# Halves of the first stage moved beside the third stage, the bias sum moved ahead of the difference, and the seam's casts moved

## The chip, the core and the metric

One core of one Trainium2 chip runs the program. The metric is the device time of one execution in microseconds (us); the median of several executions is compared.

## The reference

```python
X = np.fft.rfft(x, axis=1)                    # x: 8 x 3072 x 256
Yr = Xr @ w_r - Xi @ w_i + b_r                # 256 x 256 weights
Yi = Xr @ w_i + Xi @ w_r + b_i
Y = softshrink(Yr, 0.01) + 1j * softshrink(Yi, 0.01)
y = np.fft.irfft(Y, n=3072, axis=1)           # -> 24576 tokens x 256
h = y @ w_in                                  # 256 x 2048
g = where(h >= 1, h, where(h <= -1, 0, (h + 1) ** 2 / 4))
out = g @ w_out                               # 2048 x 256
```

## The kernel before

The Fourier transform of length 3072 is done as 48 x 64, as matmuls with constant matrices. **First stage** (`stage1`, line 213): a "half" is four rows of one batch; four small matmuls on quarters of the array write banks A and B (one buffer each), and two ScalarE copies (line 228) take them to `zst`, which SyncE stores to `z_d` with four transfers (`store_z`, line 230). **Second stage** (`stage2`, line 246) and **mixing** run in units: `UN` = 96 units, `NU` = 12 a batch. Second-stage matmuls write a bank of tag D (two buffers). ScalarE copies the imaginary part (`split_X_hi`, line 270) and casts the whole to `Xh` (`round_X`, line 277). VectorE forms the difference in place (`difference`, line 294), ScalarE casts it to `Xdh` (line 312), VectorE forms the low parts `Xl` (line 306) and `Xdl` (line 313). `mix_shared` (six matmuls) and `mix_rest` (twelve) multiply by the weights into a bank of tag C (two buffers; all of line 320). Between them VectorE adds `bias_i` to the shared part (`take_shared`, line 336; in the first unit of a batch also one row, line 338), and afterwards adds the sum to the bank (`add_bias`, line 350). ScalarE and VectorE shrink the result (`above`, line 355; `shrink`, line 359). **Third stage** (`stage3`, line 378, matmuls of line 368): one for two units, in odd units, into the two banks of tag E, copied by ScalarE (line 382) and stored to `u_d`. **Fourth stage** (`stage4`, line 488, `half4`): back to tokens, through banks A and B, eight parts for the first batch beside the unit loop, with ScalarE copies (line 516). Operands of the feed-forward part are cast by `prep_split_hi` (ScalarE) and `prep_split_lo` (VectorE, line 560), in four parts; part 0 and 1 come from the fourth stage's output, 2 and 3 from sums on GpSimd.

The unit loop is lines 767 to 856, and the order of each engine's queue is the order of the calls (`manual_schedule`). In iteration u stand: `mix_shared(u-2)`, `difference(u-1)` and its casts, `take_shared(u-2)`, `above(u-3)`, `Xl` and `Xdl` of u-1, `shrink(u-3)`, one weight step, in odd u `stage3(u-5)`, the halves of this unit, a part of the fourth stage if u is in `U4`, one weight step, `stage2(u)` and its copies, `mix_rest(u-2)`, one weight step, `add_bias(u-2)`. At the head of the iteration SyncE issues the stores of the halves done so far, `load_z(u+2)` and one `load_x`.

Weight steps (`weight_steps`, line 468) turn float64 weights to pairs of float32 numbers from unit 12 on, three steps a unit, so that one of 32 tiles takes two units. In even units they are the VectorE steps of lines 415, 420 and 422 and two ScalarE steps (418, 419); in odd units those of lines 424 and 426, a GpSimd product (431) and the split of the tile before (`split_weights`, line 437): for every second one of the first 16 a ScalarE cast of `winh` (line 465) and a GpSimd subtraction (466), for each of the last 16 a cast of `wout` (line 443).

Which halves fall due comes from these lines; an even unit takes one of those due, an odd unit leaves one:

```python
lo, hi = (min(NH, NJ + (max(0, k - 1) if k <= NJ else NJ + 2 * (k - NJ) // 3)) for k in (u, u + 1))
hs_u = due[: 1 if not odd else max(0, len(due) - 1)]
```

Of the kernel before, what the change touches and what calls it, by code (L numbers as in the profile page):

```python
# [103 lines left out]
def tile_fft_mix_moe(  # L104
    ctx: ExitStack, tc: tile.TileContext, x, x_first, w_r, w_i, b_r, b_i, w_in, w_out, c1, c2, t_f, t_i, out
):
    nc = tc.nc
# [7 lines left out]
    NU = G // 2  # L115
# [48 lines left out]
    def split(eng, hi, lo, src):  # L164
        eng.tensor_copy(hi, src)
        eng.tensor_tensor(out=lo, in0=src, in1=hi.bitcast(F32), op=ALU.subtract)
# [46 lines left out]
    def stage1(h, tags, copies):  # L213
        a = xin.pop(h)
        ps = [pools["ps"].tile([P, HT, D], F32, tag=k, bufs=2 if k == "C" else 1, name="ps_f1") for k in tags]
        for k, e in QUARTERS:
            rows = slice(k * HP, k * HP + R1)
            nc.tensor.matmul(  # L218
                ps[k][e * HP : (e + 1) * HP],
                lhsT=c1_sb[rows, Q:],  # L220
                rhs=a[rows, e * HT : (e + 1) * HT, :],
                start=True,
                stop=True,
                tile_position=(k * HP, e * HP),
            )
        for k, copy in enumerate(copies):
            z = zst[h, k] = first_st.tile([P, HT, D], F32, tag="zst", bufs=5, name="zst")
            copy(z, ps[k])
# [31 lines left out]
    def both(ps):  # L260
        return (ps[:, :, c].rearrange("p d g s -> p d (g s)") for c in range(2))

    def split_X_hi(u):
        ps = xp[u]
        _, im = both(ps)
        if u == 0:
            dp[u] = fold.tile([P, 2, D], F32, tag="yb", name="im")[:, :, :P]
        else:
            dp[u] = mixing.tile([P, ND, P], F32, tag="Xd", name="Xd")
        nc.scalar.copy(dp[u], im)  # L270
        if u > 0:
            round_X(u)

    def round_X(u):
        ps = xp[u]
        hi = mixing.tile([P, ND, 2, 2, R2], F32R, tag="Xh", bufs=2, name="Xh")
        nc.scalar.copy(hi, ps)
        xp[u] = ps, hi
# [19 lines left out]
    def split_first(u):  # L298
        if u in first_col:
            e = first_col.pop(u)  # L300
            split(nc.vector, *(a[:, :, 0:1] for a in e0), e)
# [32 lines left out]
    def take_shared(u):  # L334
        ps = yp[u]
        nc.vector.tensor_tensor(out=shift[:, 1, :], in0=ps[:, 0, :], in1=bias_i, op=ALU.add)
        if u % NU == 0:
            nc.vector.tensor_tensor(out=shift[0:1, 1, :], in0=ps[0:1, 0, :], in1=shift[0:1, 0, :], op=ALU.add)
# [173 lines left out]
    def stage4_out(c, copies):  # L512
        hb, m = divmod(c, JH // JT)
        to = yt[hb][:, :, :, m * JT : (m + 1) * JT].rearrange("p d (r h) j -> p d r h j", h=2)
        for h, (copy, ps) in enumerate(zip(copies, ps4.pop(c), strict=True)):
            copy(to[:, :, :, h, :], ps.rearrange("p d j r -> p d r j"))

    def bank(tag, bufs=1):
        return pools["ps"].tile([P, 2, BANK // 2], F32, tag=tag, bufs=bufs, name="ps_i2")
# [21 lines left out]
    def split_slices(i, part):  # L541
        hb, k = divmod(i, NK)
        if part == 0:
            sl, src = slice(0, 1), halves_of(i)[0][0].rearrange("p q j -> p (q j)")
        elif part == 1:
            sl, src = slice(1, 3), yt[hb][:, 1, k * QT : (k + 1) * QT, :].rearrange("p q j -> p (q j)")
        else:
            at = 2 * part - 4
            sl, src = slice(3 + at, 5 + at), raw_t[i][:, at : at + 2].rearrange("p o q j -> p (o q j)")
        return src, *(a[:, sl, :].rearrange("p o n -> p (o n)") for a in ops[i])  # L550

    def prep_split_hi(i, part):
        if part == 0:
            ops[i] = [pools[f"ops{i % 2}"].tile([P, 7, TH], F32R, tag=f"op{k}", name=f"op{k}") for k in "hl"]
        src, hi, lo = split_slices(i, part)
        nc.scalar.copy(hi, src)

    def prep_split_lo(i, part):
        src, hi, lo = split_slices(i, part)
        nc.vector.tensor_tensor(out=lo, in0=src, in1=hi.bitcast(F32), op=ALU.subtract)  # L560
        if part == 3:
            del raw_t[i]
            if i % NK == NK - 1:
                del yt[i // NK]
# [115 lines left out]
    UN = B * NU  # L680

    def halves(u):

        lo, hi = (min(NH, NJ + (max(0, k - 1) if k <= NJ else NJ + 2 * (k - NJ) // 3)) for k in (u, u + 1))
        return range(lo, hi)
# [7 lines left out]
    with tc.manual_schedule():  # L693
# [61 lines left out]
        def half4(tags="AB"):  # L755
            c = next(four4)
            stage4(c, [bank(k, 2 if k == "D" else 1) for k in tags])
            stage4_out(c, [nc.scalar.copy] * 2)

        U4 = (UN - 8, UN - 6, UN - 4, UN - 3, UN)  # L760

        U_IN = UN - NU + 2

        WU = 12
        due = []
        used = NX + 1
        for u in range(UN + 3):
            odd = u % 2
            due.extend(h for h in halves(u) if h > NX + 1)
            hs_u = due[: 1 if not odd else max(0, len(due) - 1)]  # L770
            del due[: len(hs_u)]
            at = lambda lag: 0 <= u - lag < UN
            weights = more_weights if WU <= u < 85 else lambda: None
            while (stored, 0) in zst:
                store_z(stored)
                stored += 1
            if at(6) and not odd:
                store_u(u - 6)
            if u == NU:
                wout = keep.tile([P, NF, 2, D], F32R, tag="wout", name="wout")  # L780
            if 0 < u < NU - 3:
                load_t(2 * u + 6, 2 * u + 8)
            if 0 < u <= NU:
                load_ti(u - 1)
            if u == WU - 1:
                load_weights(0)
                load_weights(1)
            if u == 10:
                nc.sync.dma_start(c2_sb, c2)
            if NU <= u + 2 < UN:  # L790
                assert stored >= NJ * ((u + 2) // NU + 1)
                load_z(u + 2)
            if xs < min(NH, used + AHEAD):
                load_x(xs)
                xs += 1
            if at(2):
                mix_shared(u - 2)
            if u == 2:
                take_shared(0)
                split_first(0)  # L800
            if at(1):
                difference(u - 1)
                rest = split_difference(u - 1)
                if u == 1:
                    round_X(0)
            if at(2) and u > 2:
                take_shared(u - 2)
            if at(3):
                above(u - 3)
            if at(1):  # L810
                if u > 1:
                    split_X_lo(u - 1)
                rest()
                if u == 1:
                    split_X_lo(u - 1)
                    first_col[0] = minus_sum(*first_col[0])
                else:
                    split_first(u - 1)
            if at(3):
                shrink(u - 3)  # L820
            weights()
            if at(5) and odd:
                stage3(u - 5)
            for h in hs_u:
                stage1(h, "AB", [nc.scalar.copy] * 2)
                used += 1
            if u in U4:
                half4()
            weights()
            if u == UN + 1:  # L830
                half4("DD")
            if u < UN:
                stage2(u)
                split_X_hi(u)
            if u == 1:
                stage1(NX + 1, "AB", [nc.scalar.copy] * 2)
                used += 1
            if at(2):
                mix_rest(u - 2)
                weights()  # L840
                add_bias(u - 2)
            if u == U_IN:
                assert not due and stored == NH
                for _ in ws:
                    pass
                first_st.release()
                pools["in"] = right("in")
                pools["in"].tile([P, 24], F32, name="edge")
                pools["ops0"] = right("ops0")
                for c in range(2):  # L850
                    load_u(c)
            if u == UN - 2:
                prep_sums(0)
            for part in {UN - 2: (0,), UN - 1: (1,), UN: (2, 3)}.get(u, ()):
                prep_split_hi(0, part)
                prep_split_lo(0, part)
        mixing.release()
        pools["ops1"] = right("ops1")
        pools["ps"].release()
# [21 lines left out]
        for n in range(NUNIT):  # L881
            i, p = divmod(n, NP)
            part = p - 4 if i + 1 < NT and p >= 4 else None
# [137 lines left out]
```

## Time and profile before

| | before |
|---|---|
| median of 3 runs | 2567.1 us (2567.05 to 2567.39) |
| the profiled execution | 2565.8 us, its span 2564.0 us |
| TensorE busy | 2553.1 us (100% of the span) |
| VectorE busy | 2061.7 us (80%) |
| ScalarE busy | 1693.1 us (66%) |
| GpSimd busy | 133.5 us (5%) |
[...]

The unit loop fills the first 490 us of the span; the feed-forward part (lines 881 to 974) the rest. In the profile PE is TensorE, PEld its weight load, DVE VectorE, ACT ScalarE, POOL GpSimd and SP SyncE. Busy times are taken over whole spans, and an engine's queue is followed in a timeline. Matmuls overlap, and their ends are modelled; so TensorE's time is read from the starts.

### The profile page before, as it was taken

What the parts mean: (1) busy time and instruction counts of PE and PEld (TensorE: products, weight loads), DVE (VectorE), ACT (ScalarE), POOL (GpSimd) and SP (SyncE); (2) the same over time, 40 slices, a digit from 0 to 9 for tenths busy, and PEclk for the clock granted to TensorE, in tenths of its full rate; (3) what the DMA queues carried; (4) which work ended last, traced back from release to release, by engine and by line L of the source; (5) the groups of instructions that cost most, each with busy time, mean ns of one, the idle gap of its engine ahead of it and who ended that gap; (6) DMA issues with size and microseconds to landing.
All of it is one profiled execution on the core that took longest, in us unless ns stands there. A gap on an engine that the chain in (4) does not pass through costs nothing.

```text
span 2564.0 us, 48556 instructions
## 1 busy us (share of the span) xinstructions
PE 2553.1 (100%) x19512; PEld 2459.6 (96%) x19512; DVE 2061.7 (80%) x3246; ACT 1693.1 (66%) x2713; POOL 133.5 (5%) x144
## 2 busy tenths in 40 slices
PE   9999999999999999999999999999999999999998
PEld 8888888899999999999999999999999999999998
DVE  5788886688888888888888888888888888888886
ACT  6777776666666666666666666666666666666665
POOL 2243320000000000000000000000000000000000
PEclk9999999999999999999999999999999999999999
DMA  9988775300111111111111111111111111111001
GB/s 247 276 243 241 236 228 157 113 13 13 26 26 26 26 26 26 26 26 26 26 26 25 25 25 25 25 25 25 25 25 25 25 25 25 25 25 25 13 15 23
DMA packets 195345, 160.30 MB, mean 63 GB/s; under 512 B 117296, under 2 KB 167088, under 8 KB 195120
## 3 DMA queue, kind: packets, MB, share of 16 engines
q1 hardware_dynamic: 193312, 156.73, 24.8%
q8 instruction: 153, 2.51, 0.4%
q10 hardware_dynamic: 1808, 0.48, 0.1%
q14 instruction: 72, 0.59, 0.1%
HBM read 84.78 MB, written 72.35 MB: 61 GB/s over the span
## 4 chain that ended last, share of the span: by engine, by line
PE 98%; DMA 1%; DVE 0%; ACT 0%; issue 0%; SPq 0%
PE acc L644 41%; PE ps_X L583 16%; PE ps_Y L583 10%; PE ps_mix L320 8%; PE ps_Z L583 5%; PE ps_V L583 5%; PE ps_f L252 4%; PE ps_i L368 4%; PE ps_i L501 2%; PE ps_f L218 2%; DMA xin<-in_x 0%; DMA t_sb<-in_t 0%; DMA xin<-in_x_first 0%; DVE h L617 0%; DVE h L602 0%
## 5 line engine op out<-in xcount | busy, mean ns | idle before, releaser
L644 PE MATMUL acc<-gh,wout 128*128 128x384 f32 x4096 | 1202.4, 334 | 0.0
L644 PEld LDWEIGHTS acc<-gh,wout 128*128 128x128 f32 x4096 | 754.0, 188 | 0.0
L612 ACT ACTIVATE r<-h,half 128x768 f32<-128x768 f32 x512 | 481.5, 940 | 368.9 <-DVE h L602 368.9
L644 PE MATMUL acc<-gl,wout 128*128 128x384 f32 x2048 | 684.0, 334 | 0.1
L627 DVE TENSOR_TENSOR gl<-h,gh 128x768 fp32r<-128x768 f32 x512 | 488.7, 955 | 113.1 <-ACT gh L622 85.2
L596 ACT COPY snap<-ps_X 128x384 f32<-128x384 f32 x768 | 370.0, 482 | 301.7 <-PE ps_X L583 301.0
L617 DVE SCALAR_TENSOR_TENSOR h<-h,r 128x768 f32<-128x768 f32 x512 | 486.8, 951 | 32.2 <-ACT r L612 0.3
L622 ACT CAST gh<-h 128x768 fp32r<-128x768 f32 x512 | 429.3, 839 | 1.4 <-DVE h L617 1.4
L602 DVE CUSTOM_DVE_ANT_0 h<-ps_Y,snap 128x384 f32<-128x384 f32 x512 | 283.4, 554 | 128.4 <-PE ps_Y L583 128.2
L644 PEld LDWEIGHTS acc<-gl,wout 128*128 128x128 f32 x2048 | 384.4, 188 | 0.5 <-DVE gl L627 0.5
L583 PE MATMUL ps_X<-oph,winh 128*128 128x384 f32 x768 | 260.3, 339 | 0.6 <-ACT snap L596 0.6
L583 PE MATMUL ps_X<-opl,winh 128*128 128x384 f32 x768 | 256.6, 334 | 0.0
L583 PE MATMUL ps_X<-oph,winl 128*128 128x384 f32 x768 | 256.6, 334 | 0.0
L602 DVE CUSTOM_DVE_ANT_0 h<-ps_Z,snap 128x384 f32<-128x384 f32 x256 | 142.3, 556 | 103.5 <-ACT snap L596 103.4
L583 PE MATMUL ps_Y<-oph,winh 128*128 128x384 f32 x512 | 171.1, 334 | 0.1
L583 PE MATMUL ps_Y<-oph,winl 128*128 128x384 f32 x512 | 171.0, 334 | 0.0
L583 PE MATMUL ps_Y<-opl,winh 128*128 128x384 f32 x512 | 171.0, 334 | 0.0
L583 PEld LDWEIGHTS ps_X<-oph,winh 128*128 128x128 f32 x768 | 144.1, 188 | 3.5 <-ACT snap L596 1.6
L583 PEld LDWEIGHTS ps_X<-opl,winh 128*128 128x128 f32 x768 | 144.2, 188 | 0.0
L583 PEld LDWEIGHTS ps_X<-oph,winl 128*128 128x128 f32 x768 | 144.1, 188 | 0.0
L350 DVE TENSOR_TENSOR y<-ps_mix,shift 128x512 f32<-128x512 f32 x96 | 66.3, 690 | 95.5 <-PE ps_mix L320 95.4
L602 DVE CUSTOM_DVE_ANT_0 h<-ps_V,snap 128x384 f32<-128x384 f32 x256 | 139.9, 546 | 0.0
(124 smaller groups left out, 3789.5 us busy)
## 6 DMA issues: line engine op xcount, KB each, us to landing
uin<-u_d SPq DMA_DIRECT2D x128, 192.0 KB, 4.1
out<-ot SPq DMA_DIRECT2D x504, 48.0 KB, 2.0
u_d<-ust SPq DMA_DIRECT2D x47, 512.0 KB, 3.6
xin<-in_x SPq DMA_DIRECT2D x112, 192.0 KB, 4.3
z_d<-zst SPq DMA_DIRECT2D x224, 96.0 KB, 2.5
zin<-z_d SPq DMA_DIRECT2D x84, 256.0 KB, 3.8
wraw<-in_moe_w_in SPq DMA_DIRECT2D x16, 256.0 KB, 4.9
wraw<-in_moe_w_out SPq DMA_DIRECT2D x16, 256.0 KB, 4.5
```

The costliest lines, as they stand in the source:

```text
L252: nc.tensor.matmul(ps[:, d, :, gi, :], lhsT=z[:, gi, d * P : (d + 1) * P], rhs=t_sb[:, 2 * v + gi, :].rearrange("p (c s) -> p c s", c=2), ...
L320: nc.tensor.matmul(out, lhsT=a[:, d], rhs=wm[nm, k][:, d, :], start=start and n == 0, stop=n == 3 * ND * len(pairs) - 1, skip_group_check= ...
L350: nc.vector.tensor_tensor(out=y, in0=yp[u], in1=shift, op=ALU.add)
L368: nc.tensor.matmul(ps[gi][:, k, :], lhsT=ti_sb[rows, v + k, c, :], rhs=y[rows, c, :], start=c == 0 and k == 0, stop=c == 1, tile_position= ...
L583: nc.tensor.matmul(ups[to], lhsT=win[a][p][:, w, :], rhs=mv[:, m, :], start=start and k == 0, stop=k == 2, skip_group_check=True,)
L596: nc.scalar.copy(snaps[n][:, at, :], ups["X"])
L602: nc.vector._custom_dve(TENSOR_ADD_SAT, out=hs[n][:, to, :], in0=ups[a], in1=snaps[n][:, at, :], s0=FLT_MAX, s1=-1.0)
L612: nc.scalar.activation(rs[n][:, of(f)], hs[n][:, of(f)], AF.Square, bias=half, scale=0.5)
L617: nc.vector.scalar_tensor_tensor(out=h, in0=h, scalar=1.0, in1=r, op0=ALU.max, op1=ALU.min)
L622: nc.scalar.copy(gs[n, f][0], hs[n][:, of(f)])
L627: nc.vector.tensor_tensor(out=gl, in0=hs[n][:, of(f)], in1=gh.bitcast(F32), op=ALU.subtract)
L644: nc.tensor.matmul(acc[i, q], lhsT=wout[:, 2 * p + f, a, e * P : (e + 1) * P], rhs=gs[n, f][k][:, 1 - t, :], start=p == 0 and f == 1 and ( ...
```

## The change

It touches the unit loop alone. From unit 12 (`NU`) on, an even unit takes no halves and an odd unit takes all that are due. Where there is more than one, the first goes ahead of the third stage, and the others stay behind it. In even units from 12 on `take_shared` goes ahead of `difference`. The first-batch parts of the fourth stage move from units 88, 90, 92, 93, 96 to 89, 91 (one ahead of the third stage and one behind it), 93 and 96. Of the operand casts at the end of the loop, the ScalarE cast of part 1 goes ahead of `round_X` in unit 95, the VectorE cast of part 1 to unit 96 and those of parts 2 and 3 to unit 97.

```diff
@@ split_X_hi
         nc.scalar.copy(dp[u], im)
+        if u == UN - 1:
+            prep_split_hi(0, 1)
         if u > 0:
             round_X(u)
@@ unit loop
-        U4 = (UN - 8, UN - 6, UN - 4, UN - 3, UN)
+        U4 = (UN - 7, UN - 5, UN - 3, UN)
+        prep_lo = {UN: (1,), UN + 1: (2, 3)}
...
-            hs_u = due[: 1 if not odd else max(0, len(due) - 1)]
+            late = u >= NU
+            hs_u = due[: (0 if not odd else len(due)) if late else (1 if not odd else max(0, len(due) - 1))]
...
+            if at(2) and late and not odd:
+                take_shared(u - 2)
             if at(1):
                 difference(u - 1)
                 rest = split_difference(u - 1)
...
-            if at(2) and u > 2:
+            if at(2) and u > 2 and (odd or not late):
                 take_shared(u - 2)
...
             weights()
+            if late and len(hs_u) > 1:
+                stage1(hs_u.pop(0), "AB", [nc.scalar.copy] * 2)
+                used += 1
+            if u == UN - 5:
+                half4()
+            if u in prep_lo:
+                for part in prep_lo[u]:
+                    prep_split_lo(0, part)
             if at(5) and odd:
                 stage3(u - 5)
...
-            for part in {UN - 2: (0,), UN - 1: (1,), UN: (2, 3)}.get(u, ()):
+            for part in {UN - 2: (0,), UN: (2, 3)}.get(u, ()):
                 prep_split_hi(0, part)
-                prep_split_lo(0, part)
+                if part == 0:
+                    prep_split_lo(0, part)
```

## Rows read from the trace of the kernel before

**Rows 1.** Windows view: stretch, length, busy us of each engine, clock, DMA.
```profile
300.00:400.00 100.00, 100.00 (x812) 81.21 (x805) 82.50 (x180) 72.12 (x148) 29.23 (x30) 1.00 0.74 218
```
**Rows 2.** Timeline of PE, 330 to 345: start us, length us, engine, line, operation.
```profile
333.09 0.28 PE L320 MATMUL ps_mix<-wm_ih,Xdh 128*128 128x256 f32 x1
...
338.23 0.28 PE L320 MATMUL ps_mix<-wm_ih,Xdh 128*128 128x256 f32 x1
...
339.03 1.09 PE L218 MATMUL ps_f<-xin,c_sb 48*64 48x512 f32 x8
...
342.47 0.28 PE L320 MATMUL ps_mix<-wm_ih,Xdh 128*128 128x256 f32 x1
```
**Rows 3.** Timeline of PE in an even unit with neither half nor third stage.
```profile
417.06 0.28 PE L320 MATMUL ps_mix<-wm_ih,Xdh 128*128 128x256 f32 x1
...
417.77 1.05 PE L252 MATMUL ps_f<-t_sb,zin 128*128 128x128 f32 x8
418.67 0.39 PE L320 MATMUL ps_mix<-wm_bh,Xh 128*128 128x256 f32 x1
...
420.19 0.28 PE L320 MATMUL ps_mix<-wm_ih,Xdh 128*128 128x256 f32 x1
```
**Rows 4.** Timeline of PE in an odd unit: third stage, half, second stage.
```profile
284.23 2.00 PE L368 MATMUL ps_i<-y,ti_sb 64*128 64x256 f32 x16
286.16 1.09 PE L218 MATMUL ps_f<-xin,c_sb 48*64 48x512 f32 x8
287.18 1.16 PE L252 MATMUL ps_f<-t_sb,zin 128*128 128x128 f32 x8
```
**Rows 5.** Timeline of DVE in the even unit of rows 2; in brackets idle time before.
```profile
338.43 0.69 DVE L350 TENSOR_TENSOR y<-ps_mix,shift 128x512 f32<-128x512 f32 x1 [0.57 <-PE ps_mix L320]
339.04 0.41 DVE L294 TENSOR_TENSOR Xd<-ps_f,Xd 128x256 f32<-128x256 f32 x1
339.37 0.41 DVE L336 TENSOR_TENSOR shift<-ps_mix,bias_i 128x256 f32<-128x256 f32 x1
...
340.63 0.68 DVE L359 SCALAR_TENSOR_TENSOR y<-y,over 128x512 f32<-128x512 f32 x1
...
341.76 0.29 DVE L422 TENSOR_SCALAR scl<-scl 128x256 uint32<-128x256 uint32 x1
342.68 0.69 DVE L350 TENSOR_TENSOR y<-ps_mix,shift 128x512 f32<-128x512 f32 x1 [0.62 <-PE ps_mix L320]
```
**Rows 6.** Timeline of ACT in the same even unit and the odd one behind it.
```profile
339.80 0.72 ACT L355 ACTIVATE over<-y,lam 128x512 f32<-128x512 f32 x1
...
343.73 0.41 ACT L312 CAST Xdh<-Xd 128x256 fp32r<-128x256 f32 x1 [0.59 <-DVE Xd L294]
...
344.67 0.39 ACT L443 CAST wout<-both 128x256 fp32r<-128x256 f32 x1
```
**Rows 7.** Timeline of ACT: a first-column unit, a `winh` cast, and a half's copies.
```profile
255.21 0.41 ACT L312 CAST Xdh<-Xd 128x256 fp32r<-128x256 f32 x1 [0.98 <-DVE Xd L296]
...
158.46 0.92 ACT L465 CAST winh<-wpair 128x896 fp32r<-128x896 f32 x1
...
287.30 1.08 ACT L228 COPY zst<-ps_f 128x512 f32<-128x512 f32 x2
```
**Rows 8.** Timelines of POOL and of DVE at 139 us.
```profile
139.50 2.16 POOL L466 TENSOR_TENSOR winl<-wpair,winh 128x896 fp32r<-128x896 f32 x1 [4.54 <-ACT winh L465]
...
139.58 2.22 DVE L424 TENSOR_SCALAR scl<-scl 128x256 uint32<-128x256 uint32 x1
```
**Rows 9.** Timeline of PE: units 86 and 96.
```profile
434.30 1.05 PE L252 MATMUL ps_f<-t_sb,zin 128*128 128x128 f32 x8
435.64 0.39 PE L320 MATMUL ps_mix<-wm_bh,Xh 128*128 128x256 f32 x1 [0.29 <-DVE shift L338]
...
483.79 0.39 PE L320 MATMUL ps_mix<-wm_bh,Xh 128*128 128x256 f32 x1 [1.17 <-DVE shift L336]
```
**Rows 10.** Timeline of SP: the issue of one half's four stores.
```profile
287.91 1.72 SPq L236 DMA_DIRECT2D z_d<-zst  x4
```

## The prediction

> **What bounds the kernel now.** Read the stretches first, then the timelines of one pair of units, engine by engine. In the unit loop TensorE is busy all the time while VectorE and ScalarE have room [rows 1], so a unit lasts as long as what TensorE issues in it. I set every unit's zero at the first matmul of `mix_shared` on TensorE. In a pair with one half in its even unit, the odd unit takes 338.23 − 333.09 = 5.14 us and the even one 342.47 − 338.23 = 4.24 us [rows 2]. After the last half is done, an even unit holds neither half nor third stage and takes 420.19 − 417.06 = 3.13 us [rows 3]. So a half in an even unit costs 1.11 us. In an odd unit, behind the third stage, it costs 287.18 − 286.16 = 1.02 us [rows 4]. The other engines follow: in each even unit VectorE waits 0.62 us and in each odd one 0.57 us for TensorE [rows 5]. That idle time is the cover of everything below, and the change takes most of it away in the even units.
>
> **The gains.** The formula in `halves` gives 47 halves from unit 12 on. Before, 35 lie in even units and 12 behind a third stage. After, 35 lie behind a third stage (or behind one another) and 12 just ahead of one. 35 halves thus cost 1.02 instead of 1.11: −3.2 us. No row shows a half followed by the third stage. Ends: 1.02 us, as behind it [rows 4], and 0.93, without the 0.09 us that a matmul group takes longer before a half (0.80, rows 2) than before the second stage (0.71, rows 3). I take 1.02, since the third stage itself is no shorter before a half (1.93 us, rows 4); the other end would be worth 12 × 0.09 = 1.1 us. [...] Three parts of the fourth stage also go from even to odd units: −0.3 us at the same 0.09 each. At the seam TensorE waits 1.17 us for the bias sum [rows 9], because the low part of an operand cast stands ahead of the difference and the sum on VectorE and itself waits for its ScalarE part. The change takes the ScalarE part ahead of `round_X`, the VectorE part behind `shrink`, and the sum ahead of all of them: −1.2 us. The later casts then run in unit 97 on VectorE while TensorE does third and fourth stage; without that cover they would cost their own length, as now. Gains: −4.7 us.
>
> **The bias sum.** It can start when `mix_shared` has landed. Results land 0.21 us after the next group starts (342.68 − 342.47, rows 2, 5), so at 0.71 + 0.21 = 0.92 us. In a short even unit `mix_rest` starts at 418.67 − 417.06 = 1.61; the sum ends in time. Every twelfth even unit has a second, one-row sum behind it. The one short unit of this kind that exists now delays `mix_rest` to 435.64 − 434.30 = 1.34 us behind the second stage instead of 0.90, a wait of 0.44 [rows 9, 3]. The sum comes 0.22 us sooner after the change (0.92 against 339.37 − 338.23 = 1.14, rows 2, 5), which leaves 0.22, but now in seven units: 7 × 0.22 − 0.44 = +1.1 us.
>
> **The lag that the short even unit makes.** Ahead of it, the sum puts `difference` back from 0.81 to 0.92 + 0.33 = 1.25 us (the 0.33 from 339.04 to 339.37, rows 5), that is by 0.44. ScalarE's cast of the difference and `above` move with it: `above`, now from 1.57 to 2.29 [rows 6], ends at 2.73, and `shrink` can start at 2.80 instead of 2.40 [rows 5]. Behind it stand the three weight steps, which end at 3.82 now [rows 5] and so at 4.22 then. `add_bias` is due at 3.13 + 0.21 = 3.34. VectorE is 0.88 us late at the start of each odd unit while weights are converted (units 12 to 75). In an odd unit with one half this is harmless: the unit grows by 1.02, VectorE's idle time is 0.57 + 1.02 − 0.88 = 0.71 us, and the half's banks have been free since the last pair.
>
> **The stall.** An odd unit with two halves now has one ahead of the third stage and one behind it, both in banks A and B, one buffer each. The second can start only when ScalarE has copied out the first. In the odd unit's clock TensorE is ready for it at 0.80 + 1.02 + 1.93 = 3.75 us. ScalarE works in order: cast of the difference, `above`, the weight cast, and only then the two copies. It is through with `above` at 344.67 − 342.47 = 2.20 [rows 2, 6], with the lag at 3.08. Two copies take 1.08 us [rows 7]; with 0.05 to the matmul, the banks are free at 4.2 without a weight cast, at 4.5 with that of `wout` (0.39 us, 0.3 of it before the next start, rows 6), and at 5.0 with that of `winh` (0.92, so 0.8, rows 7). The waits are 0.45, 0.75 and 1.25 us. In units where u − 1 is a multiple of 12 the first column is done too, and the cast of the difference waits 0.98 instead of 0.59 us [rows 7, 6]: +0.39. By the code's counts the units are: 19, 31, 43 (no cast, but a `winh` unit just before, where VectorE ends late [rows 8]: taken as 0.6 each, 1.8); 55, 67 (`wout`, 1.5); 49, 61, 73 (`wout` and first column, 1.14 each, 3.4); 25, 37 (`winh`, first column, and GpSimd beside VectorE ahead of it, some 0.3: 1.95 each, 3.9). Unit 13 has three halves, two of them back to back: 0.45 + 0.39, and then copies that start 1.14 us after the half (287.30 − 286.16, rows 4, 7) and end 1.08 later against 1.02 of matmul, another 1.25: 2.1. Unit 79 has no weights, so no lag: free at 3.3, no wait. Together 12.7 us. Ends: zero, if the copies come 0.5 to 2 us sooner than this, and half as much again, 19 us.
>
> SP sends eight stores ahead of `load_z` after such a unit instead of four, 1.72 us more [rows 10]. That load is wanted two units later, some 9 us on, so I cost it at nothing; without that cover it would be up to 1.7 us in each of ten pairs.
>
> **The sum.** −4.7 + 1.1 + 12.7 = +9.1 us. On the profiled execution (2565.8, its span 2564.0) this is 2574.9. The median of the runs, 2567.1, lies 1.3 above that execution, so 2576.
>
> **Rivals.** (a) The first half's copies are out before the third stage ends. Then what is left is −4.7 + 1.1, 2563.5, or 2562.4 with the cheaper order of half and third stage: the case on the other side. It decides where ScalarE is free for the copies by 2.6 us of the odd unit instead of 3.1 to 4.3. For it: without the lag it would be free at 2.2, so that unit 79 fits. Against it: VectorE has 0.62 us of idle time in an even unit that loses 1.11, and the moved sum adds 0.40 of waiting. (b) VectorE doesn't catch up in the odd units and sets the pair. Its work is 9.38 − 0.62 − 0.57 = 8.2 us, with the new waits 8.6, against 9.3 of TensorE; it decides from 0.7 us more a pair. GpSimd can do that in places: a weight step took 2.22 us beside a GpSimd subtraction of 2.16 that began just before it [rows 8]. At 1.0 us more a pair in all 32 pairs it would be 32 × 0.3, near 2586. [...] (c) The stalls are there but half as long, since ScalarE reaches the copies sooner than by my worst-case order: 2570.
>
> **Chances.** Forecast 0.6, (a) 0.18, (b) 0.07, (c) 0.15. A difference of 0.2%, 5.1 us, is about what can be told from no change: faster means under 2562.0, slower over 2572.2. (a) lies on the lower edge, so I give it 0.1 to faster and 0.08 to same; (c) gives 0.12 to same; the rest is slower. The forecast's own range is 2572 to 2581. For 8 in 10 it reaches down into (a) and a little over the top: 2563 to 2583.
>
> **What would show it.** In odd units 19, 25, … 73 TensorE stands idle ahead of the second half, released by ScalarE's copy of the first, 0.4 to 2 us each; in 79 it doesn't. `add_bias` of an even unit starts some 0.9 us late while weights are converted, without idle time before it. An even unit takes 3.13 us, a pair with one half about 9.27. The wait of 1.17 us at the seam is gone. No idle time ahead of second halves would make the prediction wrong, and then rival (a) holds; idle time ahead of `mix_shared` in every pair would mean (b).

## The result: 0.9% slower, and the profile after

The changed kernel takes 2589.82 us (median of 5 runs, 2588.01 to 2591.28), the kernel before 2567.1 us. The ratio is 1.0087, with a 95% interval of 1.0073 to 1.0102. The profiled execution took 2590.05 us with a span of 2587.9 us, 23.9 us more than before. The forecast was 2576 us with a range up to 2583: slower was right, but the time lies above the range, and the loss is two and a half times the forecast one.

First the windows view of after, which answers to [rows 1]: stretch, length, busy us of PE, PEld, DVE, ACT and POOL, granted clock, DMA share, GB/s.

```profile
100.00:200.00 100.00, 94.80 (x749) 77.54 (x747) 79.84 (x166) 65.53 (x131) 39.01 (x45) 0.98 0.84 226
200.00:300.00 100.00, 94.88 (x750) 76.45 (x749) 79.70 (x172) 66.16 (x137) 32.79 (x35) 0.98 0.82 224
300.00:400.00 100.00, 96.90 (x789) 79.15 (x787) 83.45 (x176) 68.24 (x145) 29.98 (x30) 1.00 0.82 228
```

The first two stretches before, beside [rows 1]:

```profile
100.00:200.00 100.00, 100.00 (x813) 81.24 (x812) 86.21 (x181) 72.93 (x145) 42.48 (x46) 1.00 0.83 244
200.00:300.00 100.00, 100.00 (x814) 81.86 (x816) 85.30 (x180) 72.40 (x147) 36.09 (x38) 1.00 0.82 242
```

TensorE, which had no idle time in these stretches before, now idles 3 to 5 us in each hundred, and in the first two the granted clock is 0.98 (0.997 over the whole span, 0.999 before). The view of waits of PE in after says on whom: engine, line, tile, then whom it waited for, us in total, times, longest.

```profile
PE ps_f L218 <- ACT zst L228: 13.7, 12, 2.2
PE ps_mix L322 <- DVE shift L338: 2.6, 6, 0.5
PE ps_mix L322 <- DVE shift L340: 1.1, 7, 0.2
```

Twelve waits of halves for ScalarE's copies are the stall of the forecast: ten second halves and the two further halves of unit 13. The six waits for the bias sum (line 336 before, 338 now) were not in it. These idle times are lower bounds, because a half that has started with bank A still waits for bank B inside: the second half of unit 55 below takes 1.57 us, the first 1.09. So I took the length of each unit from the starts of the first matmul of `mix_shared` in the PE timeline of both traces, as in [rows 2, 3]:

| unit | before, us | after, us | what it holds |
|---|---|---|---|
| even, 16 | 4.24 | 3.02 | no half any more |
| even, 22 (and 18, 30, 34, 42, 46) | 4.24 | 3.71 | the same, behind a unit with the `winh` cast |
| even, 14 (and 26, 38, 50, 62, 74) | 4.93 | 4.14 | the same, first unit of a batch |
| odd, 57 | 5.14 | 6.16 | one half |
| odd, 79 | 6.16 | 7.18 | two halves, no weight steps |
| odd, 19, 31, 43 | 6.16 | 8.31 | two halves, no weight cast |
| odd, 55, 67 | 6.16 | 8.57 | two halves, `wout` |
| odd, 49, 61, 73 | 6.16 | 8.97 | two halves, `wout`, first column |
| odd, 25, 37 | 6.16 | 11.46 | two halves, `winh`, first column |
| odd, 13 | 6.16 | 14.32 | three halves, first column |

Unit 79 has two halves and no weight steps, and has no stall. Its 7.18 us is the yardstick: every odd unit with two halves and weight steps is 1.1 to 4.3 us longer.

The timelines of unit 55 (it starts at 304.98) show how a stall is made. PE, DVE, ACT of after:

```profile
305.77 1.09 PE L218 MATMUL ps_f<-xin,c_sb 48*64 48x512 f32 x8
306.79 2.00 PE L370 MATMUL ps_i<-y,ti_sb 64*128 64x256 f32 x16
309.64 1.57 PE L218 MATMUL ps_f<-xin,c_sb 48*64 48x512 f32 x8 [0.85 <-ACT zst L228]
311.14 1.16 PE L252 MATMUL ps_f<-t_sb,zin 128*128 128x128 f32 x8
...
305.42 0.29 DVE L417 TENSOR_SCALAR man<-wraw 128x256 uint32<-128x256 uint32 x1
...
305.94 0.29 DVE L424 TENSOR_SCALAR scl<-scl 128x256 uint32<-128x256 uint32 x1
306.15 0.68 DVE L352 TENSOR_TENSOR y<-ps_mix,shift 128x512 f32<-128x512 f32 x1
307.32 0.42 DVE L296 TENSOR_TENSOR Xd<-ps_f,Xd 128x256 f32<-128x256 f32 x1 [0.49 <-ACT Xh L279]
...
305.80 0.42 ACT L420 ACTIVATE parts<-man 128x256 f32<-128x256 f32 x1 [1.02 <-DVE man L417]
306.12 0.43 ACT L421 ACTIVATE parts<-wraw 128x256 f32<-128x256 uint32 x1
306.46 0.35 ACT L270 COPY Xd<-ps_f 128x256 f32<-128x256 f32 x1
306.71 0.58 ACT L279 CAST Xh<-ps_f 128x512 fp32r<-128x512 f32 x1
307.78 0.40 ACT L314 CAST Xdh<-Xd 128x256 fp32r<-128x256 f32 x1 [0.49 <-DVE Xd L296]
308.10 0.72 ACT L357 ACTIVATE over<-y,lam 128x512 f32<-128x512 f32 x1
308.72 0.39 ACT L445 CAST wout<-both 128x256 fp32r<-128x256 f32 x1
309.01 1.06 ACT L228 COPY zst<-ps_f 128x512 f32<-128x512 f32 x2
```

`add_bias` (L352) starts 306.15 − 304.98 = 1.17 us into the unit instead of 0.21: the lag, 0.88 forecast and 0.96 measured. The next step was not in the forecast. The difference (L296) does not follow at once but waits 0.49 us for ScalarE's cast `Xh`, which stands behind the two weight steps of ScalarE (L420 and L421), and these wait 1.02 us for a step of the late VectorE (L417). So ScalarE comes to the copies at 309.01 − 304.98 = 4.03 us instead of 3.4. Without a wait the second half would start at 306.79 + 1.93 = 308.72 and the second stage 1.02 later, at 309.74; it starts at 311.14, 1.40 us late.

### The profile page after: what moved, and what is told of

It reads as the page before. It is cut to its first block, busy times and chain, and to the rows that moved or that the text cites. A ratio compares the mean times of both kernels' runs of the same rounds, so it can differ in the third digit from the quotient of the medians.

```text
span 2587.9 us, 48493 instructions
## 1 busy us (share of the span) xinstructions
PE 2560.7 (99%) x19512; PEld 2465.5 (95%) x19512; DVE 2066.8 (80%) x3246; ACT 1688.1 (65%) x2713; POOL 132.6 (5%) x144
## 4 chain that ended last, share of the span: by engine, by line
PE 92%; DVE 3%; ACT 2%; DMA 1%; issue 1%; SPq 0%; ACTq 0%; DVEq 0%
PE acc L646 41%; PE ps_X L585 16%; PE ps_Y L585 10%; PE ps_mix L322 5%; PE ps_Z L585 5%; PE ps_V L585 5%; PE ps_f L252 3%; PE ps_i L503 2%; PE ps_i L370 2%; PE ps_f L218 2%; DMA zin<-z_d 1%; PE ps_f L196 1%; DVE y L352 1%; ACT over L357 0%; DVE shift L338 0%
## 5 line engine op out<-in xcount | busy, mean ns | idle before, releaser
L352 DVE TENSOR_TENSOR y<-ps_mix,shift 128x512 f32<-128x512 f32 x96 | 66.0, 687 | 91.8 <-PE ps_mix L322 91.3
```

The source lines that it names most:

```text
L352: nc.vector.tensor_tensor(out=y, in0=yp[u], in1=shift, op=ALU.add)
```

## The experiments

My theory was that of the forecast: in the short even unit the weight steps make VectorE late, through it ScalarE, so the copies of the half ahead of the third stage come late. The rivals: two halves beside one third stage are dear in themselves; the moved bias sum makes the lag; the lag costs by itself, with or without second halves. All edits below are to after (to before where said), and unit lengths are taken as above.

**The weight steps moved out of the even units.**

```diff
-            weights()
+            if not late:
+                weights()
...
-            weights()
+            for _ in range(3 * odd if late else 1):    # behind the halves, and again behind mix_rest
+                weights()
```

> As after, but from unit 12 on all six weight steps of a tile stand in the odd unit (three behind the halves, three behind mix_rest), none in the even one. Theory (the weight steps make VectorE, and through it ScalarE, late in the short even units, so the copies of the half ahead of the third stage come late): the lag goes, the waits ahead of second halves in units 19 to 73 go (1.1 to 2.7 us each in after), those on the bias sum in even units 18, 22, 30, 34, 42, 46 too; unit 13 keeps about 1.25 us for its two halves back to back. Time near 2561 to 2563. Rival (two halves beside the third stage in one unit are dear in themselves): no change, near 2590. Rival (the moved bias sum makes the lag): it is still ahead, so most of the loss stays, over 2580.

Measured: 2582.11 us (ratio to before 1.0062, 1.0046 to 1.0079). The even units behind a `winh` unit are short (22: 3.01), but second halves still wait (55: 8.06 us; 19: 9.11, where `mix_shared` waits 0.64 us for `Xdl` too). The expectation missed, and the timelines of POOL and DVE in unit 54 (it starts at 293.14) say why:

```profile
295.89 1.35 POOL L433 TENSOR_TENSOR both<-parts,scl 128x512 f32<-128x512 f32 x1
...
296.01 1.77 DVE L361 SCALAR_TENSOR_TENSOR y<-y,over 128x512 f32<-128x512 f32 x1
297.71 0.68 DVE L352 TENSOR_TENSOR y<-ps_mix,shift 128x512 f32<-128x512 f32 x1
```

The weight steps left VectorE's queue in the even unit, but GpSimd's share, which follows them, fell into it. `shrink` takes 1.77 us beside the GpSimd product instead of 0.68 [rows 5], and `add_bias` of unit 54 starts 297.71 − 296.16 = 1.55 us into the odd unit, later than in after. So this run doesn't free VectorE and can't refute the theory; here too a late `add_bias` goes with waits ahead of second halves. Odd units with one half grow as well (23: 7.66 us, 53: 6.60, instead of 6.16). The time also meets the condition of the rival of the moved sum, over 2580; what decides that one is the run without the moved sum, below.

**The cast `Xh` ahead of the weight steps of ScalarE.**

```diff
+            if odd or not late:
                 weights()
...
                 stage2(u)
                 split_X_hi(u)
+            if late and not odd:
+                weights()
```

> As after, but in even units from 12 on the middle weight step (two ScalarE steps and one of VectorE) stands behind the copy and the cast of the second stage instead of ahead of them. Theory (the difference of the odd unit starts only after the cast Xh, which stands behind those two ScalarE steps): the 0.49 us that VectorE waits ahead of the difference go, the wait ahead of each second half is some 0.5 us shorter (11 units), units 25 and 37 may keep full clock: 2580 to 2585. Rival (dear in themselves): no change. Rival (the moved sum): no change.

Measured: 2573.97 us (1.0033, 1.0019 to 1.0046), better than expected. DVE, ACT and PE in unit 55 (it starts at 291.50):

```profile
292.67 0.68 DVE L352 TENSOR_TENSOR y<-ps_mix,shift 128x512 f32<-128x512 f32 x1
293.27 0.41 DVE L296 TENSOR_TENSOR Xd<-ps_f,Xd 128x256 f32<-128x256 f32 x1
...
291.58 0.59 ACT L279 CAST Xh<-ps_f 128x512 fp32r<-128x512 f32 x1
292.32 0.42 ACT L420 ACTIVATE parts<-man 128x256 f32<-128x256 f32 x1 [0.15 <-DVE man L417]
...
295.58 1.57 PE L218 MATMUL ps_f<-xin,c_sb 48*64 48x512 f32 x8 [0.27 <-ACT zst L228]
```

`add_bias` is as late as in after (1.17 us), but the difference follows it at once. Units 19 and 31 go from 8.31 to 7.71, 55 and 67 from 8.57 to 8.00, 49, 61 and 73 from 8.97 to 8.38: 0.6 us each, as the wait for `Xh` and its echo. The six even units behind `winh` go from 3.71 to 3.10 but for unit 18 (3.42). Units 25 and 37 go from 11.46 to 8.92, 2.5 us, and unit 13 from 14.32 to 10.33; more on these below.

**ScalarE's weight cast behind the copies.**

```diff
-            weights()
             if late and len(hs_u) > 1:
                 stage1(hs_u.pop(0), "AB", [nc.scalar.copy] * 2)
                 used += 1
+            weights()
```

> As after, but where a half stands ahead of the third stage, the unit's first weight step (with the ScalarE cast of wout or winh) stands behind it instead of ahead. Theory (ScalarE works in order and the copies wait behind the cast): the wait ahead of the second half is 0.3 us shorter in units 49, 55, 61, 67, 73, 0.8 us in units 25 and 37, unchanged in 19, 31, 43; without the longest wait the clock may stay at full speed in 25 and 37, another 1.5 us each: 2583 to 2587. Rival (dear in themselves): no change anywhere, 2590.

Measured: 2580.78 us (1.0058, 1.0043 to 1.0073). Units 55 and 67: 8.28, 0.29 less; 49, 61, 73: 8.66, 0.31 less; 19, 31, 43 unchanged (8.31). Units 25 and 37: 9.05, 2.4 less. This follows the theory unit by unit, in the place that the edit touches and in no other, but for unit 13 (10.86), where it changes nothing in the order of ScalarE's work. The 3.5 us that unit 13 loses are not the edit's. In the profiled execution of after, VectorE's first weight step waited for its transfer, which put the second half 0.68 us later into the unit (80.89 − 75.52 = 5.37 against 80.89 − 76.20 = 4.69), and from the third half on TensorE ran at a granted clock of 0.51, called half clock below. The step in after, then the windows from the third half to the end of unit 13, first of after, then of cast_behind (the same 28 groups on PE):

```profile
76.63 0.29 DVE L417 TENSOR_SCALAR man<-wraw 128x256 uint32<-128x256 uint32 x1 [0.59 <-DMA wraw<-in_moe_w_in]
...
83.13:89.84 6.71, 6.71 (x28) 4.89 (x29) 0.00 (x0) 1.96 (x4) 1.11 (x2) 0.51 0.78 226
...
83.14:87.06 3.92, 3.92 (x28) 2.81 (x29) 0.00 (x0) 1.02 (x2) 1.10 (x2) 1.00 0.94 239
```

**Both edits together.** The two diffs above.

> As after, with both edits of parts_behind and cast_behind. Theory (the waits add up on ScalarE's queue, so the savings do too): against parts_behind 0.3 us less in units 49, 55, 61, 67, 73 and 0.8 in 25 and 37, 3 us in all: near 2571. Rival (they overlap): as parts_behind, 2574.

Measured: 2571.24 us (1.0018, 1.0008 to 1.0027). Units 55 and 67: 7.70, 49, 61, 73: 8.08, 25 and 37: 8.10. The savings add up, so both sit on the one queue. What is left over the 7.18 of unit 79 is 0.5 us in 55.

**The bias sum behind the difference.**

```diff
-            if at(2) and late and not odd:
-                take_shared(u - 2)
...
-            if at(2) and u > 2 and (odd or not late):
+            if at(2) and u > 2:
```

> As after, but the bias sum stands behind the difference in even units again, as in before. Theory: VectorE's lag is some 0.4 us shorter, so the waits ahead of second halves are 0.4 us shorter (11 units, -4.4), while the second stage of each short even unit waits 0.1 us for the sum (+3.9) and that of every twelfth 0.2 us more: 2588 to 2592. Rival (the moved sum makes the lag): the loss goes, under 2575.

Measured: 2583.12 us (1.0069, 1.0054 to 1.0084), better than expected; the rival would have been under 2575. Unit 55 goes from 8.57 to 7.99 and 49 from 8.97 to 8.39, 0.6 us, as the lag is shorter; short even units grow from 3.02 to 3.13. The moved sum is a part of the lag, not its cause, and without second halves it is worth 0.11 us in each short unit. The expectation did not name all that moved. In the profiled execution (2586.59 us, the longest of the four) unit 13 takes 10.29 us and unit 37 9.48, both with a granted clock of 1.00 behind their waits, while unit 14 grows from 4.14 to 7.50. There the bias sum, behind the difference again, shares its wait for `Xh` (2.25 us, behind the last copy of unit 13's third half), and TensorE waits 2.63 us for it.

**Two halves in unit 13 instead of three.**

```diff
-            hs_u = due[: (0 if not odd else len(due)) if late else (1 if not odd else max(0, len(due) - 1))]
+            hs_u = due[: (0 if not odd else len(due)) if late else (1 if not odd else len(due) if u == NU - 1 else max(0, len(due) - 1))]
```

> As after, but unit 11 takes all halves that are due, so that unit 13 has two and not three. Theory: unit 13 goes from 14.3 to about 8.7 us and keeps full clock, unit 11 grows by 1.0: 4 to 5 us faster than after, near 2585. Rival (the half clock in unit 13 comes from its edge work and not from the waits): the slow stretch stays, 2 us faster at most.

Measured: 2586.34 us (1.0074, 1.0060 to 1.0087). Unit 13 goes from 14.32 to 8.61 (granted clock 1.00), unit 11 from 5.15 to 6.16. That is as expected, 4.7 us in these two. But unit 49 is now 10.53 us instead of 8.97, with the same wait (1.25 and 1.24 us); see the section on the hardware.

**No half ahead of the third stage.**

```diff
-            if late and len(hs_u) > 1:
-                stage1(hs_u.pop(0), "AB", [nc.scalar.copy] * 2)
-                used += 1
```

> As after, but no half stands ahead of the third stage: where an odd unit has two, both stand behind it. Theory (the second waits for the copies of the first, now behind the copy of the third stage on ScalarE as well): the wait ahead of the second half is 0.5 to 1.5 us longer than in after in each of 11 units, half clock in more of them: 2595 to 2615. Rival (the place ahead of the third stage is itself what costs): under 2590.

Measured in a single execution: 2609.42 us, as expected, where the rival would have been under 2590. Unit 55 is 9.50 us, 0.93 more than in after, and unit 79, which had no stall, is 8.43 instead of 7.18. In the PE timeline of unit 55 the two halves stand back to back:

```profile
319.76 1.09 PE L218 MATMUL ps_f<-xin,c_sb 48*64 48x512 f32 x8
322.62 1.57 PE L218 MATMUL ps_f<-xin,c_sb 48*64 48x512 f32 x8 [1.77 <-ACT zst L228]
```

The place ahead of the third stage is the better one: it gives ScalarE 1.9 us. Unit 79 shows the price of two halves back to back without any lag, 8.43 − 7.18 = 1.25 us, which was the forecast's own term.

**Never more than one half in a unit.**

```diff
-            hs_u = due[: (0 if not odd else len(due)) if late else ...]
+            hs_u = due[: (int(len(due) + len(halves(u + 1)) > 1) if not odd else len(due)) if late else ...]
```

where two would fall into an odd unit, the even one ahead takes one, and unit 11 takes all that are due.

> As after, but where two halves would fall into an odd unit the even unit ahead takes one of them, and unit 11 takes all that are due: no odd unit has more than one half. Theory: no waits ahead of second halves, no half clock; pairs with one half 0.2 us shorter than in before, every twelfth even unit 0.4 us longer than the others, even units 22, 34, 46 some 0.7: near 2565. Rival (the lag of the short even units costs by itself, also without second halves): 2575 or more.

Measured: 2565.82 us (0.9995, 0.9986 to 1.0004). No odd unit is longer than 6.17 us, and the waits for ScalarE's copies and the half clock are gone (granted clock 1.00 in every window from 70 to 400 us). Against after this is 24 us. So the lag costs little without second halves (2.6 us from unit 11 to 81, by the next run): the rival of the lag by itself falls, and so does "dear in itself", with unit 79. But from unit 11 to 81 it is no faster than before (345.9 against 344.9 us): even units 22, 34 and 46 are still 3.71 to 3.76 us, and 26 and 38 4.72 to 4.74.

**Spread, with the cast `Xh` ahead of the weight steps in short units.**

```diff
+            short = late and not odd and not hs_u
+            if not short:
                 weights()
...
                 split_X_hi(u)
+            if short:
+                weights()
```

> As spread, but in even units without a half the middle weight step stands behind the second stage's copy and cast, as in parts_behind. Theory (those two ScalarE steps hold back Xh, it the difference, and that the bias sum of the next short even unit): even units 22, 34, 46 go from 3.7 to 3.1 us and 26, 38 from 4.7 to 4.1: 3 us under spread, near 2563, the first version that is clearly under before. Rival (spread's gain is eaten elsewhere): within 1 us of spread.

Measured: 2563.2 us (0.9984, 0.9976 to 0.9993). Units 22, 34 and 46 are 3.12 us; 26 is 4.36, so there it gives less than expected. From unit 11 to 81 it takes 343.25 us.

**And without the one-row sum.**

```diff
+    bias_e = first_st.tile([P, D], F32, name="bias_e")
...
-        nc.vector.tensor_tensor(out=shift[:, 1, :], in0=ps[:, 0, :], in1=bias_i, op=ALU.add)
-        if u % NU == 0:
+        edge = u % NU == 0 and u > 0
+        nc.vector.tensor_tensor(out=shift[:, 1, :], in0=ps[:, 0, :], in1=bias_e if edge else bias_i, op=ALU.add)
+        if u == 0:
...
+            if u == 6:
+                nc.vector.tensor_copy(bias_e, bias_i)
+                nc.vector.tensor_copy(bias_e[0:1], shift[0:1, 0, :])
```

> As spread_parts, but the one-row sum of every twelfth unit is gone: a second copy of the bias with that row already in it is made once in unit 6. Theory (the second sum holds mix_rest back by 0.4 us in units 14, 26, 38, 50, 62, 74, 86): 2 to 3 us under spread_parts, near 2560.5. Rival (those units are long for their extra matmuls alone): no change.

Measured: 2559.19 us (0.9973, 0.9964 to 0.9981): faster than both kernels, 8 us under before and 31 under after. Units 14, 50, 62 and 74 go from 4.14 to 3.71, so the second sum cost 0.43 us each. Its windows view shows TensorE without idle time again:

```profile
100.00:200.00 100.00, 100.00 (x819) 81.10 (x818) 85.77 (x183) 74.99 (x148) 41.14 (x46) 1.00 0.93 259
200.00:300.00 100.00, 100.00 (x824) 82.86 (x823) 85.75 (x180) 72.73 (x148) 36.24 (x38) 1.00 0.88 241
```

**The seam alone, on before.** The new `U4`, the three moved casts and the part ahead of the third stage in unit 91; `late = False` leaves halves and bias sum as they were.

> Before with the moved casts at the seam and the moved parts of the fourth stage alone; halves and bias sum as before. Theory: the wait of 1.17 us in unit 96 goes and three parts of the fourth stage cost 0.1 to 0.2 us less each, so 1.5 to 2 us faster: 2565.0 to 2565.6. Rival (the later casts hold back the start of the feed-forward part): no faster than before.

Measured: 2565.32 us (0.9991, 0.9982 to 1.0000). By the starts, the stretch from unit 81 to 97 takes 71.9 us instead of 73.4, 1.5 less; in after, with the moved sum as well, 71.1. From unit 11 to 81 it takes 344.85 us, as before. The interval of the ratio ends at no change, so it is these units that show the gain, more than the median.

weights_odd with unit 11 taking all halves due (the diff of two_in_13):

> weights_odd with unit 11 taking all halves that are due, so that unit 13 has two. Theory: about 1.2 us faster than weights_odd, near 2560, faster than before.

Measured: 2580.43 us (1.0051, 1.0038 to 1.0064). The step of 1.7 us from weights_odd is about as expected (unit 13: 7.35 instead of 9.60, unit 11 1.0 more). The time, near 2560 in the expectation, is not, for the reason that weights_odd shows.

## Why the prediction was right in kind and wrong in size

The sum of the forecast against unit lengths of after minus before:

| term | forecast, us | measured, us | worked out |
|---|---|---|---|
| 35 halves from even to odd units | −3.2 | −7.2 | 35 × (3.02 − 4.24 + 1.015) |
| waits of second halves, units 19 to 73 | +10.6 | +20.1 | 3 × 1.13 + 2 × 1.39 + 3 × 1.79 + 2 × 4.28 over 7.18 |
| unit 13 | +2.1 | +6.1 | 14.32 − (6.16 + 2 × 1.02) |
| even units behind `winh` units | 0 | +4.2 | 6 × (3.71 − 3.02), 18 a little more |
| first even units of a batch | +1.1 | +2.6 | 6 × ((4.14 − 3.02) − (4.93 − 4.24)) |
| seam and fourth stage | −1.5 | −2.3 | units 81 to 97: 71.1 − 73.4; in seam_only 71.9 − 73.4 = −1.5 |
| sum | +9.1 | +23.5 | span: +23.9, of it 0.3 ahead of unit 11 |

**Right.** The mechanism: the lag in the short even unit, ScalarE's queue, banks A and B, and the list of units. The forecast said that stalls stand in 19, 25, … 73 and not in 79, and so it is. The lag itself was 0.88 against 0.96. The seam's 1.2 us: unit 96 went from 4.63 to 3.39. A half ahead of the third stage costs 306.79 − 305.77 = 1.02 us, the end that the forecast took, and the extra stores cost TensorE nothing that the trace shows: in the view of waits of after no matmul waits for a load of `zin`. Rival (a), copies in time, didn't come about in any unit with weight steps. Of rival (b) the part on GpSimd showed, a VectorE weight step of 2.23 us beside a GpSimd subtraction of 2.20, but not in the way that it was put: VectorE caught up in every odd unit with one half except the six with a `winh` cast, which cost 4.2 us in all and not 1.0 us a pair.

**The step that failed: the lag was carried to ScalarE without the wait behind it.** "ScalarE … is through with `above` at 2.20, with the lag at 3.08." It is through at 308.72 − 304.98 = 3.74. The forecast let the difference start right behind `add_bias` and never asked when its input is free; it waits for `Xh`, which the late weight steps push back on ScalarE. So the lag feeds on itself across the two engines. In the view of waits this is the first line for before, where it could have been seen, and the second for after; parts_behind has no such line:

```profile
DVE Xd L294 <- ACT Xh L277: 2.5, 8, 0.5
...
DVE Xd L296 <- ACT Xh L279: 12.7, 26, 0.5
```

parts_behind takes the wait away and gains 0.6 us in each of these units. Across ten units this is 6 of the 9.5 us missing between 19 and 73. It leaves the lag as it is, and there the stalls come out as forecast, at a granted clock of 0.999 over the span: over the 7.18 of unit 79 each of 19, 31 and 43 is 0.53 us longer (forecast 0.6), of 55 and 67 0.82 (0.75), of 49, 61 and 73 1.20 (1.14), of 25 and 37 1.74 (1.95), and unit 13 has 10.33 − 8.20 = 2.13 (2.1). That is 12.4 us in all, against 12.7.

**The waits behind which the clock fell.** Units 25 and 37 were forecast with 1.95 us and lost 4.28. Of that 0.6 is the same failed step; the rest of their 2.3 includes some 1.6 us each of matmuls at half clock (second stage and `mix_rest` take 3.99 us in unit 25 and 4.00 in unit 37, against 2.42 in unit 25 of cast_behind), which the forecast's sum had no term for. cast_behind shows it: the edit shortens ScalarE's work by the 0.83 us of `winh` and saves 2.4 us. In unit 13 the two traces shown with cast_behind separate the 6.1 us: 6.71 − 3.92 = 2.8 us are half clock, 0.7 the late transfer of weights, and 10.86 − 8.20 = 2.7 the waits, against 2.1 forecast. So half clock cost after 2.8 + 2 × 1.6 = 6 us, as much as the failed step itself.

**The second loop of the lag.** In even units behind a `winh` unit, TensorE waits for the bias sum. The forecast used [rows 8] to add 0.15 us to the next odd unit and took the even unit's own sum to be in time. In after the long weight step (2.23 us beside GpSimd's subtraction of 2.20; 0.43 us in unit 13, while GpSimd is idle) comes later and isn't done when the even unit starts (unit 17 to 18):

```profile
107.90 2.20 POOL L468 TENSOR_TENSOR winl<-wpair,winh 128x896 fp32r<-128x896 f32 x1 [5.10 <-ACT winh L467]
...
108.16 2.23 DVE L428 SCALAR_TENSOR_TENSOR scl<-wraw,scl 128x256 uint32<-128x256 uint32 x1
110.31 0.68 DVE L352 TENSOR_TENSOR y<-ps_mix,shift 128x512 f32<-128x512 f32 x1
111.09 0.42 DVE L338 TENSOR_TENSOR shift<-ps_mix,bias_i 128x256 f32<-128x256 f32 x1
...
111.57 0.39 PE L322 MATMUL ps_mix<-wm_bh,Xh 128*128 128x256 f32 x1 [0.48 <-DVE shift L338]
```

Unit 18 starts at 109.32; the sum at 1.77 us instead of 0.92. With the difference freed (parts_behind), five of the six go to 3.10, because the long step begins and ends earlier. In that trace unit 21 starts at 120.84 and unit 22 at 127.00; the long step begins 4.28 us into the odd unit instead of 4.87 (in after 129.27 − 124.40), and the sum starts 1.09 us into the even one instead of 1.70 (132.26 − 130.56):

```profile
125.12 2.26 DVE L428 SCALAR_TENSOR_TENSOR scl<-wraw,scl 128x256 uint32<-128x256 uint32 x1
...
128.09 0.42 DVE L338 TENSOR_TENSOR shift<-ps_mix,bias_i 128x256 f32<-128x256 f32 x1
```

**Gains mis-sized.** The short even unit is 3.02 us, not the 3.13 of [rows 3]. The row already held a wait for the bias sum of 0.11 us, which the forecast read as none; sum_behind, at 3.13, shows it. It is 35 × 0.11 = 3.9 of the 4.0 us missing. The one-row sum costs 0.43 us and not 0.22, as spread_parts_bias shows. The larger gain hid a part of the missing waits.

## What to carry to other kernels

Before an engine's unit is shortened, follow the cover of every other engine in that unit, and carry a lag through all inputs of the next step, the ones on the other engine too: here a lag of 0.96 us on VectorE became 3.74 − 2.20 = 1.54 us on ScalarE, because the late VectorE held up ScalarE's cast `Xh`, which VectorE itself needed next. A single-buffered bank that is used twice in one stretch needs its copy early in the queue, ahead of anything that can wait; spreading the uses (one half a unit) was worth 24 us where tuning the queue was worth 19. A hidden wait in the row that is taken as the clean case biases the whole sum: look for a row without it.

## What the runs showed of the hardware

Behind some waits TensorE's granted clock fell. In after this is so in three stretches, behind the waits of units 13 (shown with cast_behind, 0.51), 25 and 37; the first of these lines holds the wait of unit 25 (2.15 us, to 149.40), the second is what follows, then the same for unit 37 (2.15 us, to 214.44). Windows view, columns as above:

```profile
145.00:150.00 5.00, 2.85 (x25) 1.77 (x24) 4.41 (x12) 4.12 (x10) 1.06 (x1) 1.00 0.66 187
150.00:155.00 5.00, 5.00 (x30) 4.19 (x28) 1.63 (x2) 2.22 (x5) 3.05 (x3) 0.66 0.69 199
...
210.00:215.00 5.00, 2.85 (x25) 1.73 (x24) 4.41 (x12) 4.12 (x10) 1.02 (x1) 1.00 0.67 177
215.00:220.00 5.00, 5.00 (x29) 4.19 (x28) 1.67 (x2) 2.23 (x4) 3.09 (x3) 0.66 0.61 169
```

The granted clock is 1.00 in the lines with the waits and 0.66 on average in the 5 us after them; from 152 to 154 us and from 217 to 219 us it is 0.50. In unit 25 the second stage and `mix_rest` take 154.88 − 150.89 = 3.99 us. In cast_behind, whose wait there is 1.30 us and whose clock stays at 1.00, they take 149.86 − 147.44 = 2.42. So behind a wait of 2.15 us another 1.57 us were lost.

The length of the wait alone does not decide it. In two_in_13 unit 49 idles 1.25 us, the granted clock is 0.73 in the window over it, and it takes 10.53 us. In after the same unit with the same work idles 1.24 us and takes 8.97, at a clock of 1.00. The window over unit 49 of two_in_13:

```profile
275.00:281.00 6.00, 5.19 (x27) 4.08 (x28) 2.66 (x6) 3.61 (x7) 3.22 (x3) 0.73 0.71 203
```

and of after:

```profile
275.00:281.00 6.00, 4.76 (x37) 2.81 (x33) 4.84 (x12) 4.86 (x11) 2.34 (x3) 1.00 0.84 225
```

One execution shows the same by itself. In sum_behind units 25 and 37 both wait 1.74 us ahead of the second half; unit 25 then takes 11.02 us, unit 37 9.48. The two waits, then the windows over second stage and `mix_rest` behind each:

```profile
150.42 1.64 PE L218 MATMUL ps_f<-xin,c_sb 48*64 48x512 f32 x8 [1.74 <-ACT zst L228]
214.19 1.57 PE L218 MATMUL ps_f<-xin,c_sb 48*64 48x512 f32 x8 [1.74 <-ACT zst L228]
...
151.99:155.89 3.90, 3.90 (x24) 3.90 (x21) 0.66 (x2) 1.45 (x3) 2.08 (x3) 0.59 0.70 197
215.69:218.12 2.43, 2.43 (x24) 2.43 (x22) 0.73 (x2) 1.45 (x3) 1.66 (x3) 1.00 0.37 99
```

In both pairs of rows the same wait is followed by a lower clock in one place (0.73, 0.59) and not in the other (1.00); no run here tested why. The four executions of two_in_13 lie between 2583.66 us, at a granted clock of 0.999, and 2588.36, at 0.997, the one profiled; so the loss behind unit 49 need not be in each of them. Left open: what decides in which place the clock falls behind a given wait.
